# A fixed order for all five engines in a fused attention and gated-MLP kernel, with one load and one cast moved later and the stages split into steps

## The chip, the cores and the metric

The kernel runs on one core of one Trainium2 chip. The metric is the device time of one execution in microseconds (us), taken from several runs. The engines are PE (TensorE, matrix products), DVE (VectorE), ACT (ScalarE), POOL (GpSimd) and SP (SyncE, which here only issues DMAs). The profile is one execution recorded by the hardware profiler; its span is 1.7 to 1.8 us shorter than the time of the same run. Every run also records the mean TensorE clock that the throttle granted, as a share of full speed.

## The reference, cut to what matters

```python
# q: (8 batches, 16 heads, 384, 64); k, v: 4 heads each, shared by 4 query heads
scores = q @ k.T / 8
attn   = softmax(scores)                    # per row
x      = (attn @ v) -> (8, 384, 1024)       # heads side by side
h      = relu(x @ w_in)                     # 1024 -> 1024
u, v   = h[..., :512], h[..., 512:]
v_n    = layer_norm(v)                      # over the 512
v_s    = w_spatial @ v_n + b_spatial        # mixes the 384 positions
out    = (u * v_s) @ w_out                  # 512 -> 1024
```

## The kernel before

Each batch is cut into nine visits. A visit starts with the scores of two units of 128 x 1024 and their exps on ACT; the rest of its TensorE time is filled with work of this batch and of the batch before it. `values` makes the row sums and the product with v, inverts the sums on ACT (`rec`, by Ln and Exp) and multiplies on DVE into `xt`. `do_v` is the V half with its layer norm, `do_sp` the spatial product, `do_u` the U half with the gate, `do_o` the output product. There are four PSUM tiles of 512 columns for all of them, handed out in turn (`ps`), and two double tiles for the scores. In the profiles `sums` and `X` are the PSUM tiles of `values`, and `pv`, `psp`, `pu` and `po` those of `do_v`, `do_sp`, `do_u` and `do_o`; `sc` are the scores and `aT` their exps.

```python
def values(b, qt):                     # [cut]
    sums = ps.tile(...); tiles(sums, ones)                       # PE
    nc.scalar.activation(rec, sums, AF.Ln)                       # ACT
    nc.scalar.activation(rec, rec, AF.Exp, scale=-1.0)           # ACT
    for jj in range(2):
        X = ps.tile(...); tiles(X, v16)                          # PE
        nc.vector.tensor_tensor(xt[...], X, rec, ALU.mult)       # DVE

def do_v(b, st, vector_relu=False):    # [cut] pv: 8 matmuls; v_r = relu(pv); bn_stats, bn_aggr
    if st == NST - 1:                  # layer norm of all three tiles at once
        rstd = ...                                               # ACT, Ln and Exp
        for s2 in range(NST):
            v_n = ...                                            # DVE

def first_visit(vi):                   # batch 0 [cut]
    if vi == 5:
        transpose_q(0, 1, 2)
        for gp in range(NGP): cast_k(1, gp, nc.vector)
        load_w_in(0, DH)               # U half, a casting DMA issued by GpSimd
        # ... casts of q of batch 1, tile 0, on DVE
    if vi == 6:
        values(0, 1)
        # ... casts of v and the rest of q of batch 1 on GpSimd, load_w_out()
    if vi == 7: transpose_k(1, ...); do_v(0, 0, vector_relu=True)
    if vi == 8: transpose_q(1, ..., 0); do_v(0, 1, vector_relu=True)

def visit(b, vi):                      # c = b - 1
    if vi == 0: values(c, 2); do_o(c - 1, 1)
    if vi == 1: do_o(c - 1, 2, 3)      # if b == 1 instead: cast_ws(), transposes of q
    if vi == 2: do_v(c, 2); do_o(c - 1, 4)
    if vi == 3: values(b, 0); do_o(c - 1, 5)
    if vi == 4: do_sp(c); do_u(c, 0)
    if vi == 5: do_v(b, 0)
    if vi == 6: values(b, 1); do_u(c, 1)
    if vi == 7: do_u(c, 2, 3)
    if vi == 8: do_v(b, 1); do_o(c, 0)

with tc.manual_schedule(engines={PE, POOL, SP, DVE}):
    ...                                # batch 0
with tc.manual_schedule(engines={PE, POOL, SP}):
    ...                                # batches 1 to 7 and the tail
```

An engine named in `manual_schedule` follows the order of the program. The others are put in order by a scheduler, which works across the two blocks: it drew the w_spatial cast, written in batch 1, up into batch 0.

The softmax here doesn't subtract the row's maximum and nothing guards it: scores larger than these inputs give would overflow.

## Time and profile before

Three runs gave a median of 285.35 us.

A batch is marked by the first row sums in its visits; they stand in visit 0 and belong to the last tile of the batch before.

| Part of the span (profiled run) | before |
|---|---|
| to the first row sums of batch 2 | 75.46 us |
| batches 2 to 6, each (batch 7: 29.43 us) | 29.97 us |
| from the last row sums to the end | 29.1 us |
| span | 283.9 us |

First the page of the kernel before: busy time by engine, then the busy tenths of PE, granted clock, DMA engines in 40 slices of 7.1 us. In all fences the lines are word for word, and lines between them are left out.

```profile
PE 255.3 (90%) x1957; PEld 103.9 (37%) x1957; DVE 140.3 (49%) x268; ACT 182.6 (64%) x232; POOL 43.1 (15%) x69
PE   2873188799999999999999999999999999999793
PEclk9998569979999999999999999999999999999799
DMA  8999399860032983099127933594337030103105
```

PE is full from about a quarter of the span on; the hole is in slices 4 and 5, with a reduced clock in slices 4 to 6, and DMA was full before it. The timeline of PE around the hole (start, duration, engine, line, operation, count, and in brackets the idle time before and what ended it):

```profile
33.89 0.61 PE L252 MATMUL sc<-qT,kT 64*128 64x512 f16 x2 [9.68 <-DVE qT L239]
36.77 3.57 PE L306 MATMUL pv<-w_in,xt 128*128 128x512 f16 x8 [1.47 <-DVE xt L290]
```

And that of DVE in the same stretch:

```profile
32.25 1.24 DVE L187 CAST ws<-ws 128x384 f16<-128x384 f32 x2 [13.67 <-DMA ws<-in_moe_w_spatial_dram]
33.41 0.42 DVE L239 COPY qT<-pq 128x512 f16<-128x512 f16 x1
34.66 0.90 DVE L159 CAST q<-q 128x256 f16<-128x256 f32 x4
```

PE waits for a copy (`qT`) that DVE could have made at about 20 us. DVE takes its instructions strictly in order (the Trainium skill, "TensorE: Matmul & The Clock Gate", queue-depth row of the first table, says so for VectorE and ScalarE, and this trace agrees), and in front of the copy stands the w_spatial cast, which waits 13.67 us for its data. Behind the copy stand casts of batch 1's q. The next thing to ask is when *their* data came. The DMA view of that q load, issued at about 12.4 us, says 17.2 us from issue to landing, so it arrived at about 30 us. That is the second block behind the first.

### The profile page before, as it was taken

The numbers are of one execution on the slowest core, as the hardware profiler recorded it, in microseconds if no ns is written. First come the engines' busy times: TensorE is split into PE (matmuls) and PEld (weight loads), VectorE is DVE, ScalarE is ACT, GpSimd is POOL, SyncE is SP. The second block draws the span as 40 slices with busy tenths as digits, with TensorE's granted clock in tenths as the row PEclk, the third lists the DMA queues.
The fourth block names the chain that finished last, engine by engine and source line by source line (L and its number), as shares of the span: only waits on it lengthen the run. The fifth ranks groups of instructions, "written<-read, shape, count | busy, mean of one in ns | idle before, by whom it ended". The sixth has DMA issues, their size and how long they took to land.

```text
span 283.9 us, 4758 instructions
## 1 busy us (share of the span) xinstructions
PE 255.3 (90%) x1957; PEld 103.9 (37%) x1957; DVE 140.3 (49%) x268; ACT 182.6 (64%) x232; POOL 43.1 (15%) x69
## 2 busy tenths in 40 slices
PE   2873188799999999999999999999999999999793
PEld 1321033344334343344334433443334434344351
DVE  2320465654267344744656444743583347346753
ACT  2975128648776878776886788677868777762000
POOL 2800606150000042003300150015000000000000
PEclk9998569979999999999999999999999999999799
DMA  8999399860032983099127933594337030103105
GB/s 195 273 230 266 113 214 310 227 199 3 0 148 76 223 251 134 17 218 324 48 107 173 286 91 150 141 271 136 148 94 121 2 148 32 44 0 148 76 1 222
DMA packets 57286, 41.60 MB, mean 147 GB/s; under 512 B 26800, under 2 KB 53552, under 8 KB 57264
## 3 DMA queue, kind: packets, MB, share of 16 engines
q1 hardware_dynamic: 53504, 37.89, 47.1%
q0 software_dynamic: 2720, 3.15, 6.6%
q10 hardware_dynamic: 1040, 0.26, 0.4%
q8 instruction: 15, 0.25, 0.3%
q14 instruction: 7, 0.06, 0.1%
HBM read 25.95 MB, written 12.58 MB: 136 GB/s over the span
## 4 chain that ended last, share of the span: by engine, by line
PE 81%; DMA 7%; SPq 3%; DVE 3%; ACT 3%; issue 1%; POOL 0%
PE pv L306 16%; PE pu L364 15%; PE po L389 15%; PE sc L252 12%; PE X L274 9%; PE psp L344 8%; PE sums L274 5%; DMA ws<-in_moe_w_spatial_dram 5%; SPq L122 2%; DMA q<-in_q_dram 2%; ACT aT L261 2%; DVE v_n L328 1%; DVE osb L396 0%; SPq L129 0%; DVE ws L187 0%
## 5 line engine op out<-in xcount | busy, mean ns | idle before, releaser
L261 ACT ACTIVATE aT<-sc 128x1024 f16<-128x1024 f32 x144 | 139.8, 1022 | 67.2 <-PE sc L252 67.2
L252 PE MATMUL sc<-qT,kT 64*128 64x512 f16 x288 | 46.6, 395 | 14.6 <-DVE qT L239 10.7
L306 PE MATMUL pv<-w_in,xt 128*128 128x512 f16 x192 | 47.2, 390 | 1.5 <-DVE xt L290 1.5
L290 DVE TENSOR_TENSOR xt<-X,rec 128x512 f16<-128x512 f32 x48 | 30.9, 685 | 33.4 <-ACT rec L286 30.7
L389 PE MATMUL po<-w_out,gT 128*128 128x512 f16 x192 | 47.4, 380 | 0.0
L364 PE MATMUL pu<-xt,w_in 128*128 128x384 f16 x256 | 45.8, 328 | 0.0
L319 DVE BATCH_NORM_STATS2 stats<-v_r 128x6 f32<-128x512 f32 x24 | 16.7, 695 | 49.2 <-ACT v_r L317 49.2
L274 PE MATMUL X<-aT,v 128*32 128x512 f16 x576 | 35.9, 385 | 0.0
L396 DVE COPY osb<-po 128x512 f32<-128x512 f32 x48 | 32.2, 682 | 1.5 <-PE po L389 1.5
L364 PEld LDWEIGHTS <-w_in 128*128 128x128 f16 x256 | 24.1, 99 | 22.0 <-issue 7.9
L306 PEld LDWEIGHTS <-xt 128*128 128x128 f16 x192 | 17.3, 99 | 28.3 <-issue 11.5
L389 PEld LDWEIGHTS <-gT 128*128 128x128 f16 x192 | 17.1, 97 | 26.4 <-issue 8.1
L159 POOL CAST q<-q 128x768 f16<-128x768 f32 (+2 forms) x32 | 23.4, 761 | 21.9 <-DMA q<-in_q_dram 14.9
L252 PEld LDWEIGHTS <-kT 64*128 64x128 f16 x288 | 9.8, 94 | 43.2 <-issue 30.9
L344 PE MATMUL psp<-wsT,v_n 128*128 128x384 f16 x96 | 22.8, 365 | 1.9 <-DVE v_n L328 1.5
L371 DVE SCALAR_TENSOR_TENSOR gT<-pu,v_s 128x384 f16<-128x384 f32 x32 | 17.8, 555 | 13.1 <-PE pu L364 13.1
L140 POOL CAST k<-k 128x384 f16<-128x384 f32 x13 | 6.3, 507 | 115.0 <-issue 65.3
L274 PEld LDWEIGHTS <-v 128*32 128x32 f16 x576 | 15.6, 99 | 16.5 <-issue 1.3
L351 DVE TENSOR_TENSOR v_s<-psp,bias_b 128x384 f32<-128x384 f32 x32 | 19.7, 664 | 2.8 <-PE psp L344 2.8
L274 PE MATMUL sums<-aT,ones 128*32 128x512 f16 x288 | 20.6, 393 | 0.0
L317 ACT ACTIVATE v_r<-pv 128x512 f32<-128x512 f32 x22 | 13.1, 597 | 7.0 <-PE pv L306 4.9
L328 DVE TENSOR_SCALAR v_n<-v_r,mv,rstd 128x512 f16<-128x512 f32 x24 | 11.7, 543 | 10.0 <-ACT rstd L325 10.0
(33 smaller groups left out, 95.8 us busy)
## 6 DMA issues: line engine op xcount, KB each, us to landing
out_dram<-osb SPq DMA_DIRECT2D x24, 512.0 KB, 2.7
q<-in_q_dram SPq DMA_DIRECT2D x14, 768.0 KB, 8.0
v<-in_v_dram SPq DMA_DIRECT2D x8, 384.0 KB, 9.0
k<-in_k_dram SPq DMA_DIRECT2D x7, 384.0 KB, 4.2
w_in<-in_moe_w_in_dram POOLq DMA_DIRECT2D x8, 256.0 KB, 10.0
q<-in_q_dram SPq DMA_DIRECT2D x2, 512.0 KB, 6.2
w_out<-in_moe_w_out_dram POOLq DMA_DIRECT2D x2, 512.0 KB, 7.1
ws<-in_moe_w_spatial_dram SPq DMA_DIRECT2D x1, 576.0 KB, 14.1
```

The costliest lines, as they stand in the source:

```text
L159: engine.tensor_copy(dst, src)
L252: nc.tensor.matmul(sc[:, half, :], kT[b][lo:hi, gp, t, :], rhs[lo:hi, :], start=True, stop=True)
L261: nc.scalar.activation(aT[b, qt][:, gp, t], sc, AF.Exp, scale=scale)
L274: nc.tensor.matmul(dst[32 * g : 32 * (g + 1), :], weights(t, g), a[:, g // 2, t, g % 2, :], start=(t == 0), stop=(t == NST - 1),)
L290: nc.vector.tensor_tensor(xt[:, jj, :, qt * P : (qt + 1) * P], X.rearrange("p (j q) -> p j q", j=G), rec.rearrange("p (j q) -> p j q", j=G ...
L306: nc.tensor.matmul(pv, xt[:, kc, st * P : (st + 1) * P], w_in16[:, kc, DH:DFF], start=(kc == 0), stop=(kc == NKT - 1),)
L344: nc.tensor.matmul(psp[:, 0:S], held["v_n", b, st][:, m * P : (m + 1) * P], wsT16[:, st, :], start=(st == 0), stop=(st == NST - 1),)
L351: nc.vector.tensor_tensor(held["v_s", b][:, m, :].rearrange("p (t s) -> p t s", t=NST), psp[:, 0:S].rearrange("p (t s) -> p t s", t=NST), ...
L364: nc.tensor.matmul(pu[:, 0:S], w_in16[:, kc, mu * P : (mu + 1) * P], xT[b][:, kc, :], start=(kc == 0), stop=(kc == NKT - 1),)
L371: nc.vector.scalar_tensor_tensor(held["gT", b][:, mu, :], pu[:, 0:S], 0.0, held["v_s", b][:, mu, :], op0=ALU.max, op1=ALU.mult,)
L389: nc.tensor.matmul(po, gT[:, m, tt * P : (tt + 1) * P], w_out16[:, m, half * 512 : (half + 1) * 512], start=(m == 0), stop=(m == NDT - 1),)
L396: nc.vector.tensor_copy(osb[:, half * 512 : (half + 1) * 512], po)
```

## The change

Its intent: write every engine's order by hand, split each stage into its PE, ACT and DVE steps so that they can be placed one by one, keep the w_spatial cast out of batch 0, and keep the U half of w_in out of the way of batch 1's data. Cut to its core, where unmarked lines are kept or shortened:

```diff
-    def scores / values / do_v / do_sp / do_u / do_o      (each with its PE, ACT and DVE parts)
+    def score_mm, exp, value_mm, rec, xmul, v_mm, relu, stats, rstd, norm,
+        sp_mm, sp_add, u_mm, gate, o_mm, o_copy           (one engine each)
 # batch 0
-        vi == 5: ... load_w_in(0, DH) ...
+        vi == 6: ... casts of batch 1's q and v on GpSimd, then load_w_in(0, DH); load_w_out()
-        vi == 7: transpose_k(1); do_v(0, 0)      vi == 8: transpose_q(1); do_v(0, 1)
+        vi == 7: v_mm(0, 0); relu; stats         vi == 8: transpose_k(1), transpose_q(1)
+        vi in (3, 6): exp(u0); value_mm; rec; exp(u1)     (rec ahead of the second exp)
 # batches 1 to 7 (c = b - 1, d = b - 2)
+        vi == 0: exp(u0); value_mm(c, 2); rec; exp(u1); xmul; o_mm(d, 1)
-        vi == 1, b == 1: cast_ws(); transpose_q(...)
+        vi == 1, b == 1: transpose_q(...); v_mm(0, 1); relu; stats
-        vi == 2: do_v(c, 2) with all of the layer norm; do_o(d, 4)
+        vi == 2: v_mm(c, 2); relu; stats                   b == 1: cast_ws()
-        vi == 3: values(b, 0); do_o(d, 5)
+        vi == 3: value_mm(b, 0); rec; exp(u1); rstd(c); xmul(b, 0); o_mm(d, 4)
-        vi == 4: do_sp(c); do_u(c, 0)
+        vi == 4: norm(c); exp(u1); o_mm(d, 5); v_mm(b, 0); relu; stats
-        vi == 5: do_v(b, 0)
+        vi == 5: sp_mm, sp_add x 4; u_mm(c, 0); gate
 # tail
+        rstd and norm for two tiles early, the third alone; three copies of batch 6 and every second one of batch 7 on ACT;
+        u_mm(c, 0) ahead of the spatial groups; these go to the two score tiles:
+        for m in range(NDT):
+            sp_mm(c, m, sc[m // 2][:, m % 2, :])
+            sp_add(c, m)
+        the last row of the output stored in two halves
-    with tc.manual_schedule(engines={PE, POOL, SP}):
+    with tc.manual_schedule(engines={PE, POOL, SP, DVE, ACT}):   (over all batches)
```

The order of instructions shows also that on SP the loads of the next batch now follow the first output store of a batch, not precede it.

## The prediction

> **What bounds the kernel now.** Span 283.9 us. From 75 to 254.8 us (batches 2 to 7) TensorE is solid: the table by stretches gives PE busy 28.97 of every 29 us, granted clock 1.00, 29.97 us per batch in the chain of waits. ScalarE is busy about 22, VectorE 15. Nothing the change does can be won there. The loss is at the ends.
>
> *Start.* The timeline shows PE idle 9.68 us (24.2 to 33.9) for a qT copy on VectorE. VectorE sat 13.67 us before the first w_spatial cast, a DMA landing at 32.2 us. The scheduled order is followed strictly (Trainium skill, "TensorE: Matmul & The Clock Gate", the queue-depth row: VectorE and ScalarE strict FIFO; the trace agrees, since that copy's input was ready from about 20.3 us). But removing this wait alone exposes the next ones: in the DMA issues q of batch 1 took 17.2 us to land (about 30 us) and v about 30.9, because DMA engines are saturated from 2 to 30 us at about 230 GB/s, w_in's U half among the traffic. The queue table gives 31.3% of 60 us for 3.15 MB of casting DMA: about 6.3 us of all 16 engines per 1.05 MB half. Then the clock: the same skill page (HAM clock gate) says idle windows halve the PE clock; the trace agrees, granted clock 0.50 from 28 to 40 us, so the first pv took 3.57 us instead of 1.83.
>
> *End.* The chain from 254.8 to 283.9: 2.3 us of PE idle before psp (relu, stats, rstd, three v_n in series; VectorE did two osb copies in between), and psp then took 4.1 us instead of 2.4, at reduced clock.
>
> **What the change does.** No arithmetic is removed; w_spatial's cast moves into batch 1, U's load behind batch 1's v cast on GpSimd, v of batch 0 tile 1 into batch 1, spatial matmuls one visit later, ScalarE's order becomes fixed. Without U, I put batch 1's q at about 20 to 24 us, v 22 to 25, ws 24 to 27.
>
> Batch 0 is then paced by ScalarE: exps every 0.92 us, rec 1.23 in between and now ahead of the second exp. Working the order through by hand, batch 1 starts at about 30 us (before: 43.1, with one pv of 1.8 more done). Batch 1 needs about 29.5 us of PE; U (issued about 25, landing 33 to 38, beside k, q, v of batch 2) is needed at about 44: just off the path. Batch 2 starts at about 60 instead of 75: **-15 us**.
>
> Steady batches: 29.97 again, plus 0 to 0.3 us each, as rec before exp, and relu before exp, hold back the second score of visits 1 and 4: **+1 us**.
>
> Tail: normalising two tiles early, and filling the chain with po and pu, removes the 2.3 us and the clock loss (about 1.2 us after the fill), half-store 0.2: **-3.5 us**.
>
> 285.35 - 15 + 1 - 3.5 = **268 us**; 8 in 10: 263 to 275. Faster by over 2%: 0.95; within 2%: 0.04; slower: 0.01.
>
> **What would show it.** No PE gap over 3 us after 8 us; no 0.50 clock slices from 24 to 42 us; ws cast without a long wait; batch 1's first score near 30, batch 2's near 60 us; 30.0 to 30.3 us per batch; no PE gap over 0.5 us after the last relu; span about 266.5.
>
> **What would make it wrong.** U or w_out landing after 44 us beside batch 2's loads; loads of batch b+1 now queue behind an output store on SP, so transposes could come late each batch (I see about 6 us slack); ScalarE's fixed order stalling PE more than 0.3 us per batch, which would cost up to 7 us; a colder clock in ScalarE-paced batch 0.

## More of the kernel before

The time turned out to have two levels, which the recorded clock tells apart: about 282.4 us with a mean clock of 0.975, and about 285 us with 0.962. The run profiled here is of the second.

In the steady batches the chain of waits (start, duration, what) of the kernel before, from 178.18 us on:

```profile
178.18 0.59 PE psp L344 x3
178.77 0.03 issue
178.80 1.84 PE psp L344 x9
180.64 1.39 PE pu L364 x8
```

The twelve spatial matmuls take 2.43 us here, 0.20 us each. The weight loads and DVE in the same stretch:

```profile
178.11 0.44 PEld L344 LDWEIGHTS <-v_n 128*128 128x128 f16 x4 [0.42 <-DVE v_n L328]
178.80 0.42 PEld L344 LDWEIGHTS <-v_n 128*128 128x128 f16 x3 [0.26 <-issue]
179.40 0.42 PEld L344 LDWEIGHTS <-v_n 128*128 128x128 f16 x3 [0.18 <-issue]
180.00 0.26 PEld L344 LDWEIGHTS <-v_n 128*128 128x128 f16 x2 [0.18 <-issue]
178.06 1.28 DVE L290 TENSOR_TENSOR xt<-X,rec 128x512 f16<-128x512 f32 x2
179.26 0.68 DVE L396 COPY osb<-po 128x512 f32<-128x512 f32 x1
179.86 2.39 DVE L351 TENSOR_TENSOR v_s<-psp,bias_b 128x384 f32<-128x384 f32 x4
```

The loads come in bursts 0.60 us apart, at 178.80, 179.40 and 180.00, the last two just after DVE is done with the two xt (179.34) and with osb (179.94). The four PSUM tiles go round: by the order of the program the second, third and fourth spatial group get the tiles of the two X and of the output group before, and these are free only when DVE has emptied them. PE's idle column shows nothing of it.

## The result, and the profile after

The changed kernel took 265.55 us (median of four runs, 264.31 to 265.62), the kernel before 284.97 us with the earlier runs counted in (282.70 to 285.72). The ratio is 0.932, with a 95% interval of 0.927 to 0.937. Ratios here are the mean time of one kernel's fast runs over the mean of the other's in the same rounds, so they are not quite the ratio of the medians. Executions over 1.5% slower than the fastest of the same kernel are left out of the means. The prediction, 268 us with a range of 263 to 275, holds. Its terms do not all hold.

The two profiles, part by part:

| Part of the span | before | after | change | predicted |
|---|---|---|---|---|
| to the first row sums of batch 2 | 75.46 | 59.66 | -15.8 | -15 |
| from there to the last row sums (six batches) | 179.30 | 176.30 | -3.0 | +1 |
| from the last row sums to the end | 29.1 | 26.5 | -2.6 | -3.5 |
| span | 283.9 | 262.5 | -21.4 | -17.5 |

The profiled execution before is one of the level near 285 us, with about 20.5 us at half clock (13.7 us in the hole, 3.4 us each at 57 and 265 us). A run at a mean clock of 0.975 has room for only 14.1 us of it (0.025 of 282 us, halved rate), so in those runs the two short stretches must be missing; that is worked out, and no such run of this kernel was profiled. (The profile of t1_sp_later below, with the same start and a mean clock of 0.975, has the hole and neither of the short stretches.) Against the level of 282.4 us the change is worth about 17 us: 3.0 in the steady batches, 1.2 in the tail (measured below), and so about 13 us at the start.

The profiled execution after is the fastest of its kernel, at 264.31 us. The profile of a0_after (the same kernel at 265.51 us, the usual time) reaches the first row sums of batch 2 at 60.87 us instead of 59.66. The whole difference is there by the second row sums (22.37 against 21.16 us): the 24 X matmuls at 14.6 us took 2.77 us in the one and 1.71 in the other. Comparisons of start times below therefore carry a scatter of about 1 us.

The page after, the same rows without DMA:

```profile
PE 245.9 (94%) x1957; PEld 103.2 (39%) x1957; DVE 140.6 (54%) x261; ACT 187.3 (71%) x241; POOL 43.6 (17%) x69
PE   2787798999999999999999999999999999999794
PEclk9999999999999999999999999999999999999998
```

The hole is gone and with it the slow clock. The timeline of PE after, around what was the hole:

```profile
24.59 1.90 PE L308 MATMUL pv<-w_in,xt 128*128 128x512 f16 x8
28.80 0.61 PE L250 MATMUL sc<-qT,kT 64*128 64x512 f16 x4 [0.88 <-ACT aT L259]
```

And DVE after:

```profile
19.77 0.42 DVE L239 COPY qT<-pq 128x512 f16<-128x512 f16 x1 [1.12 <-PE pq L236]
22.48 0.91 DVE L159 CAST q<-q 128x256 f16<-128x256 f32 x2 [0.55 <-DMA q<-in_q_dram]
39.62 1.85 DVE L187 CAST ws<-ws 128x384 f16<-128x384 f32 x3
```

The first pv starts at 24.59 instead of 36.77 us and takes 1.90 us instead of 3.57. The first scores of batch 1 come at 28.80 us, against 30 predicted. The q casts wait 0.55 us, because the q load now took 10.0 us to land instead of 17.2. The w_spatial cast waits for nothing.

In the steady batches the chain of waits after reads:

```profile
163.25 2.06 PE psp L356 x12
165.31 1.30 PE pu L378 x8
```

The weight loads after are one unbroken run:

```profile
163.18 1.74 PEld L356 LDWEIGHTS <-v_n 128*128 128x128 f16 x12 [0.42 <-issue]
```

Spatial groups and the first U group take 3.36 us instead of 3.85 (0.59 + 0.03 + 1.84 + 1.39). The difference of 0.49 us is that of the periods, 29.97 to 29.47.

The tail after, PE and DVE:

```profile
245.37 0.65 PE L356 MATMUL sc_sp<-wsT,v_n 128*128 128x384 f16 x3
246.06 0.66 DVE L368 TENSOR_TENSOR v_s<-sc_sp,bias_b 128x384 f32<-128x384 f32 x1 [1.69 <-PE sc_sp L356]
246.77 1.14 PE L356 MATMUL sc_sp<-wsT,v_n 128*128 128x384 f16 x6 [0.75 <-DVE v_s L368]
248.74 0.65 PE L356 MATMUL sc_sp<-wsT,v_n 128*128 128x384 f16 x3 [0.83 <-DVE v_s L368]
```

Here are two new PE gaps, 0.75 and 0.83 us, which the prediction said would not be there. The second spatial group writes the other half of a tile that the first group's add still reads.

### The profile page after: what moved, and what is told of

It reads as the page before. It is cut to its first block, busy times and chain, and to the rows that moved or that the text cites. A ratio compares the mean times of both kernels' runs of the same rounds, so it can differ in the third digit from the quotient of the medians.

```text
span 262.5 us, 4805 instructions
## 1 busy us (share of the span) xinstructions
PE 245.9 (94%) x1957; PEld 103.2 (39%) x1957; DVE 140.6 (54%) x261; ACT 187.3 (71%) x241; POOL 43.6 (17%) x69
## 4 chain that ended last, share of the span: by engine, by line
PE 86%; ACT 8%; DVE 2%; DMA 1%; issue 0%; ACTq 0%
PE po L403 17%; PE pu L378 16%; PE pv L308 16%; PE sc L250 14%; PE X L269 10%; PE sums L269 7%; ACT aT L259 6%; PE psp L356 5%; DMA q<-in_q_dram 1%; DVE v_s L368 1%; ACT rec L288 1%; PE sc_sp L356 1%; ACT rec L287 1%; PE pq L236 1%; DVE qT L239 1%; DVE ws L187 1%
## 5 line engine op out<-in xcount | busy, mean ns | idle before, releaser
L308 PE MATMUL pv<-w_in,xt 128*128 128x512 f16 x192 | 45.5, 380 | 0.0
L269 PE MATMUL X<-aT,v 128*32 128x512 f16 x576 | 35.5, 381 | 0.0
L421 DVE COPY osb<-po 128x512 f32<-128x512 f32 x42 | 28.6, 683 | 7.1 <-PE po L403 7.1
L159 POOL CAST q<-q 128x768 f16<-128x768 f32 (+2 forms) x32 | 24.2, 785 | 41.4 <-DMA q<-in_q_dram 31.2
L250 PEld LDWEIGHTS <-kT 64*128 64x128 f16 x288 | 10.7, 94 | 34.3 <-issue 30.4
L322 ACT ACTIVATE v_r<-pv 128x512 f32<-128x512 f32 x23 | 13.7, 597 | 11.4 <-PE pv L308 9.9
L368 DVE TENSOR_TENSOR v_s<-psp,bias_b 128x384 f32<-128x384 f32 x28 | 16.7, 663 | 0.0
L287 ACT ACTIVATE rec<-sums 128x512 f32<-128x512 f32 x24 | 14.4, 599 | 2.2 <-PE sums L269 2.2
L288 ACT ACTIVATE rec<-rec 128x512 f32<-128x512 f32 x24 | 15.1, 630 | 0.8
```

The lines of the kernel that those rows point to most:

```text
L159: engine.tensor_copy(dst, src)
L250: nc.tensor.matmul(sc[:, half, :], kT[b][lo:hi, gp, t, :], rhs[lo:hi, :], start=True, stop=True)
L269: nc.tensor.matmul(dst[32 * g : 32 * (g + 1), :], weights(t, g), a[:, g // 2, t, g % 2, :], start=(t == 0), stop=(t == NST - 1),)
L288: nc.scalar.activation(r, r, AF.Exp, scale=-1.0)
L308: nc.tensor.matmul(pv, xT[b][:, kc, st * P : (st + 1) * P], w_in16[:, kc, DH:DFF], start=(kc == 0), stop=(kc == NKT - 1),)
L368: nc.vector.tensor_tensor(held["v_s", b][:, m, :].rearrange("p (t s) -> p t s", t=NST), held["psp", b, m][:, 0:S].rearrange("p (t s) -> p ...
```

## The experiments

Twelve kernels ran, and all gave correct results. Runs share their rounds with the kernel before on the same chip. Where a table row reads "first sums", "period" and "tail", they are read from the profile as in the table above; the period is the mean of the five batches from batch 2 on.

| Run | median us | before, same rounds | ratio (95%) | first sums b2 | period | tail |
|---|---|---|---|---|---|---|
| s1_cast | 276.61 | 282.32 | 0.980 (0.974 to 0.987) | 67.97 | 29.97 | 27.4 |
| s2_u | 273.62 to 281.73 | 282.32 | none given | 69.69 | 29.97 | 27.4 |
| s3_both | 270.94 | 282.32 | 0.961 (0.954 to 0.968) | 62.12 | 29.97 | 27.4 |
| t1_sp_later | 285.31 | 282.32 | 1.012 (1.004 to 1.019) | 72.99 | 30.55 | 27.4 |
| t5_pe_order | 284.98 | 282.41 | 1.010 (1.004 to 1.015) | 73.88 | 30.33 | 27.4 |
| t4_before_fixed | 279.34 | 282.86 | 0.986 (0.979 to 0.993) | 68.58 | 30.36 | 27.1 |
| a0_after | 265.31 | 283.41 | 0.935 (0.930 to 0.940) | 60.87 | 29.47 | 26.5 |
| e1_mm_first | 263.66 | 283.41 | 0.929 (0.925 to 0.934) | slow profile | | |
| e2_old_tail | 266.48 | 283.41 | 0.940 (0.935 to 0.944) | 60.87 | 29.47 | 27.4 |
| t2_sp_back | 275.49 | 283.41 | 0.972 (0.966 to 0.977) | 62.26 | 30.88 | 27.5 |
| t3_free | 269.07 | 282.86 | 0.949 (0.944 to 0.955) | 63.44 | 29.47 after two longer batches | 26.6 |
| u1_u_early | 270.52 | 282.86 | 0.954 (0.948 to 0.960) | 65.76 | 29.47 | 26.5 |

### The start: is the wait that the profile names all of the loss?

**s1_cast**, the kernel before with the w_spatial cast alone moved:

```diff
 first_visit, vi == 8:
     do_v(0, 1, vector_relu=True)
+    cast_ws()
 visit, vi == 1, b == 1:
-    cast_ws()
```

> The kernel before, with the w_spatial cast alone moved to the end of batch 0's VectorE work. Theory A (two blocks in a row): VectorE no longer stops for w_spatial (landing at 32.2 us), but the casts of batch 1's q still wait for q to land at about 29.5 to 30 us, so the first pv moves from 36.8 only to about 31 to 32 us at a cold clock: about 280 us, 4 to 6 us gained. Theory B (the wait that the profile names is the whole loss): the 9.7 us gap and the slow clock both go, 271 to 273 us.

It gained 5.7 us, so the named wait was not the whole loss. The profile shows the block behind it. DVE and PE of this run:

```profile
28.78 0.50 DVE L159 CAST q<-q 128x256 f16<-128x256 f32 x2 [6.38 <-DMA q<-in_q_dram]
29.93 3.57 PE L306 MATMUL pv<-w_in,xt 128*128 128x512 f16 x8 [5.69 <-DVE xt L290]
```

DVE stands again, now 6.38 us for batch 1's q (16.4 us from issue to landing), and pv still runs at the slow clock.

**s2_u**, the kernel before with the load of the U half alone moved behind batch 1's casts:

```diff
 first_visit, vi == 5:
-    load_w_in(0, DH)
 first_visit, vi == 6, after the GpSimd casts:
+    load_w_in(0, DH)
     load_w_out()
```

> The kernel before, with the load of w_in's U half alone moved behind batch 1's casts on GpSimd. Theory A: without U, q of batch 1 lands at about 22 to 23 us and w_spatial at about 26.5, so VectorE still stops for w_spatial, but some 5.5 us shorter: first pv at about 31, about 279 us. Theory B: no effect, under 2 us, as U is not what VectorE waits for.

Its four times lie between 273.62 and 281.73 us with clocks from 0.992 to 0.967; the size of the gain is open. Its profile, of a run at 278.17 us that counts as slow, shows when w_spatial landed:

```profile
26.33 1.24 DVE L187 CAST ws<-ws 128x384 f16<-128x384 f32 x2 [7.39 <-DMA ws<-in_moe_w_spatial_dram]
```

The same wait for w_spatial, but its data came 5.9 us sooner (26.33 against 32.25), and q took 10.0 us to land instead of 17.2. The next run, whose profile is fast, has the same landing times (9.9 us for both loads), so this does not rest on a slow run alone: U's place in the queue moves both.

**s3_both**, the two edits together.

> Both moves in the kernel before. Theory A: neither block is left, batch 0 is paced by ScalarE, first pv at 24 to 26 us at full clock, about 272 us, and more than the two single gains added together (11). Theory B: as the first run alone.

It gained 11.4 us, ratio 0.961, and its first pv starts at 24.93 us, takes 1.89 us and waits 0.28 us. Theory A expected 272 and got 270.94. The line of that pv:

```profile
24.93 1.89 PE L306 MATMUL pv<-w_in,xt 128*128 128x512 f16 x8 [0.28 <-DVE xt L290]
```

Theory A expected more than the sum of the single gains, and that stays open. In first sums the single edits came 7.5 and 5.8 us sooner, and both together 13.3 us, which looks like the plain sum; but the profiles of the kernel before, of s2_u and of s3_both each have a further stretch of 3.4 us at half clock behind the hole (from 57.4, 51.2 and 43.5 us), and that of s1_cast has none.

Two edits of a few lines thus bring batch 2 to 62.12 us, and the whole change brings it to 59.66. Most of the last 2.5 us is that stretch: from the scores at 43.21 us to the U group at 47.34 us s3_both takes 4.13 us, where s1_cast, at full clock, takes 2.76 us for the same work (50.43 to 53.19), which is 1.4 us less. The rest is within the scatter of 1 us. That the new order in batches 0 and 1 gains anything more is not shown; whether it is what keeps the clock up there was not tested.

**u1_u_early**, the changed kernel with U's load put back in visit 5, ahead of batch 1's casts on GpSimd:

```diff
 first_batch, vi == 5:
+    load_w_in(0, DH)
 first_batch, vi == 6:
-    load_w_in(0, DH)
     load_w_out()
```

> The changed kernel with the load of w_in's U half put back to where it was, ahead of batch 1's q casts on GpSimd. Theory A: q of batch 1 lands at about 29 to 30 us again, the casts and transposes of batch 1 wait for it, batch 1 starts 6 to 8 us later and PE's clock falls: 272 to 275 us. Theory B (U's place does not matter once the w_spatial cast is out of the way): 265.5 us.

It took 270.52 us, 5.2 us more than the changed kernel by the medians (265.31), and first sums of batch 2 came 6.1 us later than in the profile after (4.9 us later than in that of a0_after). It was run at another time. Theory A holds, somewhat smaller than expected. DVE of this run:

```profile
28.79 0.91 DVE L159 CAST q<-q 128x256 f16<-128x256 f32 x2 [5.21 <-DMA q<-in_q_dram]
```

U has to be loaded by GpSimd because it is cast on the way (the Trainium skill, "DMA: Bandwidth & Descriptors", section "SWDGE vs HWDGE vs iDMA": a cast during a DMA only from GpSimd), and the same section says that each DMA engine takes turns between that queue and the others. The runs agree that the two slow each other (the taking of turns itself no trace shows): a q load issued at about 12.4 us lands in 16.2 to 17.2 us with U beside it and in 9.9 to 10.0 us without.

**t3_free**, the changed kernel with DVE and ACT given back to the scheduler from batch 1 on:

```diff
         first_batch()
+    with tc.manual_schedule(engines={PE, POOL, SP}):
         for b in range(1, B):
```

> The changed kernel with VectorE and ScalarE ordered by the scheduler again from batch 1 on (batch 0 stays fixed). The listing shows nearly the same order, save that the scheduler draws the w_spatial casts up into batch 0 again, ahead of the xt products. Theory A (fixing the order is worth little but for that cast): w_spatial lands at about 26.5 us, so VectorE stands about 3 us, of which 1 to 2 us reach the end: 266.5 to 267.5 us; period 29.5. Theory B (fixing all five engines is what carries the change): over 5 us slower.

269.07 us, 3.8 us more than the changed kernel, twice to four times what theory A expected and less than theory B. Against the profile of a0_after 2.6 us of it is at the start (first sums of batch 2 at 63.44 against 60.87) and 1.2 us in batches 2 and 3 (30.30 and 29.86 us); from batch 4 on the period is the same 29.47. The scheduler drew the cast up again, and DVE stood for it:

```profile
26.53 1.81 DVE L187 CAST ws<-ws 128x384 f16<-128x384 f32 x3 [3.11 <-DMA ws<-in_moe_w_spatial_dram]
28.99 0.38 PE L236 MATMUL pq<-ident,q 128*128 128x128 f16 x4 [1.70 <-DVE xt L296]
```

What the expectation missed is that xt was behind the cast and xt's PSUM tile was what the transposes needed. The clock then fell as well: it was 0.50 from 32.1 to 35.5 us, and the row sums at 32.34 us took 1.47 us instead of 0.83. Fixing the order by hand mattered for where that cast stands. For the steady batches it was not needed: there the period with the scheduler is the same, 29.47 us.

### The steady batches: what made them shorter?

**t1_sp_later**, the kernel before with the spatial product one visit later and nothing else:

```diff
-        if vi == 4: do_sp(c); do_u(c, 0)
-        if vi == 5: do_v(b, 0)
+        if vi == 4: do_v(b, 0)
+        if vi == 5: do_sp(c); do_u(c, 0)
```

> The kernel before, with the spatial matmuls and the first U group moved one visit later, changed places with V of the next tile, and nothing else. Theory A (in the kernel before the twelve psp matmuls are paced by VectorE, which still holds their PSUM slots with xt and osb behind the layer norm): the period falls from 29.97 to 29.5 us, psp from 2.43 to 2.06 us in the chain; 282 us. Theory B (the steady gain comes from the fixed ScalarE and VectorE order): period stays 29.9 to 30.0, 285 us.

Theory A was right about the spatial groups and wrong about the period. The chain gives psp 2.06 and pu 1.30 us, exactly as in the changed kernel. But the period rose to 30.55 us. PE and DVE of this run:

```profile
175.95 1.46 DVE L328 TENSOR_SCALAR v_n<-v_r,mv,rstd 128x512 f16<-128x512 f32 x3 [1.44 <-ACT rstd L325]
177.32 1.28 DVE L290 TENSOR_TENSOR xt<-X,rec 128x512 f16<-128x512 f32 x2
178.06 0.39 PE L306 MATMUL pv<-w_in,xt 128*128 128x512 f16 x1 [0.63 <-DVE xt L290]
178.66 1.68 PE L306 MATMUL pv<-w_in,xt 128*128 128x512 f16 x7 [0.21 <-DVE xt L290]
```

V of the next tile took the place of the spatial product, and V needs xt, which stands behind three v_n on DVE. The visible PE waits alone are 0.84 us, which is more than the 0.49 us won on psp and pu.

**t5_pe_order**, the kernel before with the full TensorE order of the changed kernel in visits 2 to 5, and the old steps:

```diff
-        if vi == 2: do_v(c, 2); do_o(d, 4)
-        if vi == 3: values(b, 0); do_o(d, 5)
-        if vi == 4: do_sp(c); do_u(c, 0)
-        if vi == 5: do_v(b, 0)
+        if vi == 2: do_v(c, 2)
+        if vi == 3: values(b, 0); do_o(d, 4)
+        if vi == 4: do_o(d, 5); do_v(b, 0)
+        if vi == 5: do_sp(c); do_u(c, 0)
```

> The kernel before with the whole TensorE order of the changed kernel in the steady batches (output groups 4 and 5 moved behind the values of the next batch, V before the spatial matmuls), while VectorE and ScalarE keep the scheduler's order: rec behind the second exp, three v_n ahead of the two xt. Theory A (the shorter period needs both: the later spatial matmuls, and xt ahead of the layer norm on VectorE with rec ahead of an exp on ScalarE): counted from the trace of the run that moved the spatial matmuls alone, xt is done 1.2 us after V could start, so psp again falls to 2.06 us but the period stays at 30.3 to 30.7 us, about 285 us. Theory B (the TensorE order alone is enough, as two output groups now stand between X and V): period 29.5, 280 us.

The period is 30.33 us, within theory A's 30.3 to 30.7. PE's order alone makes the kernel 1% slower. Its chain of waits runs through ACT and DVE between two pv groups:

```profile
173.34 1.83 ACT aT L261 x2
175.17 0.18 ACT rstd L324
175.35 0.49 ACT rec L285
176.88 0.54 DVE v_n L328
177.42 1.21 DVE xt L290 x2
178.68 1.69 PE pv L306 x7
```

`rec` comes after two exps and a step of rstd; in the changed kernel it stands ahead of the second exp, rstd follows it, and xt stands ahead of v_n.

**t2_sp_back**, the changed kernel with the spatial product back in visit 4, right behind `norm`:

```diff
 visit, vi == 4:  norm(c); exp(u1); o_mm(d, 5); o_copy(d, 5)
-    v_mm(b, 0); relu(b, 0); stats(b, 0)
+    sp_mm and sp_add x 4; u_mm(c, 0); gate(c, 0)
 visit, vi == 5:  exp(u1)
-    sp_mm and sp_add x 4; u_mm(c, 0); gate(c, 0)
+    v_mm(b, 0); relu(b, 0); stats(b, 0)
```

> The changed kernel with the spatial matmuls put back to visit 4, right behind the layer norm. Theory A (the later visit is what made the steady batches shorter): at least 0.5 us more per batch, more than in the kernel before because rstd now comes behind two exps and PE stands for it: 30.0 to 31.5 us a batch, 268.5 to 276 us. Theory B (order of ScalarE and VectorE made the steady gain): period stays 29.5, 265.5 us.

275.49 us, 10.2 us more than the changed kernel in the same rounds, with a period of 30.88 us. The chain of waits now holds the layer norm: before each spatial product it runs through v_r, an exp and rec on ACT, the two xt and an output copy on DVE, then the three v_n, and only then PE:

```profile
167.46 1.94 DVE v_n L342 x3
169.45 1.80 PE psp L356 x10
```

So, against the kernel before, the later spatial product and the new DVE and ACT order each cost time alone: 0.4 to 0.6 us a batch for the TensorE order without the rest (t1, t5), and 0.9 us a batch for the rest without the TensorE order of visits 4 and 5 (t2, 30.88 against 29.97). Only together do they gain 0.5 us.

**t4_before_fixed**, the kernel before with all five engines fixed from batch 1 on and no step split:

```diff
-    with tc.manual_schedule(engines={PE, POOL, SP}):
+    with tc.manual_schedule(engines={PE, POOL, SP, DVE, ACT}):
```

> The kernel before with all five engines fixed in program order from batch 1 on, and no step split. It takes the w_spatial cast out of batch 0 (as in the run that moves it alone, 4 to 6 us gained at the start), but ScalarE now stands for VectorE's statistics before rstd, with exps queued behind it. Theory A: about 0.3 to 1 us more per batch, 280 to 285 us. Theory B (a fixed order by itself is good): period falls to 29.5, under 279 us.

279.34 us, ratio 0.986, slightly below theory A's 280 to 285 and above theory B's limit of 279. The parts agree with A: first sums 6.9 us sooner, as the cast now stands in batch 1 (at 42.0 us, without a wait; s1_cast had 7.5), and a period of 30.36 us, 0.39 us more than before. A fixed order of unsplit steps is worse in the steady batches than the scheduler's; its gain at the start is about that of moving the cast alone.

### The tail

**a0_after** is the changed kernel again, on the chip of the next three.

> The changed kernel once more, on the same chip as the three that edit it: 265.5 us, 0.932 of the kernel before.

265.31 us, ratio 0.935.

**e1_mm_first**, all four spatial groups of the tail ahead of the four adds:

```diff
         for m in range(NDT):
             sp_mm(c, m, sc[m // 2][:, m % 2, :])
+        for m in range(NDT):
             sp_add(c, m)
```

> The changed kernel, with the tail's four spatial groups all issued before the four VectorE adds. Theory A (two groups share one tile, and an add that stands between them in the program makes the second group wait for it, 0.75 and 0.83 us): both PE gaps go, 1.3 to 1.6 us gained, 264.0 us. Theory B (the PE would wait for the adds or the gates a little later anyway): under 0.5 us.

Five of its six runs took 263.06 to 263.81 us, the six of a0_after 264.43 to 265.51; they do not overlap, and the medians differ by 1.65 us (1.67 us without the slow run). Theory A holds by the times. The profiled execution took 414.52 us at a granted clock near 0.56 (see the last section), so no time can be taken from it; its order shows the twelve spatial matmuls in one run, with no wait for an add:

```profile
389.32 3.69 PE L356 MATMUL sc_sp<-wsT,v_n 128*128 128x384 f16 x12
```

This is the version that beats both kernels.

**e2_old_tail**, the changed kernel with the order of the old tail:

```diff
-        rstd(c, 0, 2); ...; norm(c, 0, 2); v_mm(c, 2); ...; rstd(c, 2, 3); norm(c, 2, 3)
-        o_mm 3, 4, 5 with copies on ACT; u_mm(c, 0); spatial groups in the score tiles
+        o_mm 1, 2, 3; v_mm(c, 2); relu; stats; rstd(c); o_mm 4, 5; norm(c)
+        spatial groups in ps tiles; u_mm and gate x 4; all copies on DVE, whole stores
```

> The changed kernel with the tail in the order of the kernel before (one layer norm over three tiles, all copies on VectorE, whole stores). Theory A: the tail grows from 26.5 to about 29 us with a PE gap of about 1.5 us before psp and psp at a lower clock: 268 us. Theory B (the new tail's gain is eaten by its two new gaps): under 1 us slower.

266.48 us, only 1.2 us slower than a0_after. The PE gap before psp is there, 1.55 us as expected, but the tail is 27.4 us and not 29, because the clock did not fall. The kernel before lost it here:

```profile
264.55 4.16 PE L344 MATMUL psp<-wsT,v_n 128*128 128x384 f16 x12 [1.52 <-DVE v_n L328]
```

with a granted clock of 0.50 from 265.6 to 269.0 us, and e2_old_tail, after a gap of the same length, did not (1.00 throughout the stretch):

```profile
246.99 2.71 PE L356 MATMUL psp<-wsT,v_n 128*128 128x384 f16 x12 [1.55 <-DVE v_n L342]
```

The same order of the tail took 27.4 us in five more traces (s1, s2, s3, t1, t5) as well. So 29.1 us belongs to the profiled execution of the kernel before, and not to its order. Nine of 32 executions of that kernel also had a mean clock of 0.962; whether they lost it in the same place was not recorded. The fair value of the new tail is 0.9 us by the traces and 1.2 us by the times, and its two gaps had eaten another 1.6 us.

## Why the prediction was right or wrong, point by point

- *"removing this wait alone exposes the next ones"*: right, and shown. s1_cast gained 5.7 us of the start and ran into the q load; s3_both took both blocks away and gained 11.4 us.
- *"Without U, I put batch 1's q at about 20 to 24 us"*: right. q landed at about 22.5 us; u1_u_early put the delay back.
- *Batch 2 at about 60 us, -15 us*: right. The first scores of batch 2 came at 59.12 us, and the first row sums 15.8 us sooner than in the profiled execution, or about 13 us against the faster level of the kernel before. The sum over the start was right; s3_both shows that the load and the cast were enough for nearly all of it.
- *"no 0.50 clock slices from 24 to 42 us"*: right, 1.00 throughout. U landed by about 39 us, against 33 to 38 predicted, and was not waited for.
- *"Nothing the change does can be won there"* and *"+1 us"* for the steady batches: wrong in sign. They gave 3.0 us. The failing step is the first reading, that PE is solid because its busy share is 28.97 of 29 us. Of every 29.97 us, 0.49 us was PE standing for a PSUM tile that DVE still held, counted as busy. The weight loads showed it before. t1_sp_later confirms that moving the spatial product frees it (2.43 to 2.06 us), and t1, t5 and t2 that it pays only together with the new DVE and ACT order. The fear of stalls from ACT's fixed order did not come true; in t4_before_fixed, where the steps are not split, the period with the fixed order is 0.39 us longer.
- *"-3.5 us"* for the tail: the mechanism was half right and the term too large. The new tail is worth 1.2 us, and 2.8 us without its gaps (e2 to e1). The 1.2 us of clock loss counted in was met in the one profiled execution and in none of the six other traces of the old tail.
- *"no PE gap over 0.5 us after the last relu"*: wrong, 0.75 and 0.83 us. The prediction did not reckon with the four spatial groups waiting for the adds, though two of them share one tile. e1_mm_first took the gaps away and gained 1.65 us.
- The sum: by the medians the measured time is 2.5 us below the point and inside the range. The steady batches were 4 us better than written and the tail about 2 us worse, so that the sum came so near is partly luck.
- Still open: why the clock falls for 3.4 us in some executions and kernels after gaps that leave it alone in others, and how much s2_u gains in time.

## What to carry to other kernels

When an engine is held up at the head of its queue, ask of the next instructions in that queue when their data came too, and price the removal of all blocks, not of the one that the profile names. A PE that is busy all the time can still be paced by the engine that empties its PSUM tiles: look for weight loads in evenly spaced bursts and compare the time per matmul with that of the same shape elsewhere. When two groups share one tile, issue both before the first reader, and before moving a stage on one engine check that what takes its place has its inputs.

## What the Trainium skill lacked or had wrong

- "TensorE: Matmul & The Clock Gate", section "Part 1: The HAM clock gate", gives one idle window of about 3.4 us before the clock halves. Here a PE gap of 1.52 us in the tail of the kernel before was followed by 0.50 about 1 us after PE had resumed, and one of 1.55 us in e2_old_tail was not. The page does say that the window is free-running, and reports elsewhere that frequent short idles make the clock fall too; it gives no length for these, and none separates the two cases here. With 9.68 us of idle the clock fell after about 2.5 us.
- I found no page that says that the clock splits the times of one single-core kernel into two levels (the page above tells only of a warm-up that varies from run to run): the kernel before took about 282.4 us at a mean clock of 0.975 and about 285 us at 0.962.
- "TensorE: Matmul & The Clock Gate" says that the ratio takes only the values 4/8 and 8/8 (and 13/16 with three busy cores). In the slow execution of e1_mm_first the clock stood at about 0.56 on one core from about 18 us to the end, 395 us long, with PE 97% busy; the page's note of a clock stuck for over 50 us comes nearest. Two rows of its page:

```profile
PE   4899999999999999999999999999999999999996
PEclk9855555555555555555555555555555555555555
```

- The same page, section "Back-to-back issue gap", gives about 131 ns per matmul for a sustained stream of weight load and matmul pairs at 512 columns. Here four po matmuls, each with its own weight load, take 0.86 us in the chain, 215 ns each, which is the page's other figure (215.7 ns, Part 1).
- In the first 16 us the granted clock in the record is 1.00 while the matmuls run at little more than half pace: twelve row-sum matmuls took 1.47 us at 13.36 us and 0.83 us at 21.16 us in the changed kernel. The same page warns in general that clock events in a trace can be unreliable; I found none that tells of this disagreement, and its cause is open.
- I found no page that says that a profile's busy PE may hide waits for a PSUM tile (0.49 us of 29.97 us here). "Perfetto Trace Analysis", in its opening note, calls matmul busy time a bad metric, because matmuls are pipelined, and points to the busy share of weight loads. Here it showed in the spacing of the weight loads, and not in their busy time (103.9 us before, 103.2 after).
